# Attention block with an MLP on one core: 128 rows of the second wo tile by an indirect load

## The chip, the core and the metric

The kernel runs on one core of a Trainium2 chip. Its engines are TensorE (PE; PEld is its weight load), VectorE (DVE), ScalarE (ACT), GpSimd (POOL) and SyncE (SP). Transfers between HBM and on-chip memory are carried out by 16 DMA engines, whichever engine issues them. The metric is the time of one execution in device microseconds (us).

## What is computed

A decode step for eight sequences with a cache of keys and values, and an MLP behind it; everything is float32.

```python
mod = (_silu(c) @ w_mod).reshape(8, 6, 1, 512)
sa, ca, ga, sb, cb, gb = (mod[:, i] for i in range(6))
h = _layernorm(x) * (1 + ca) + sa
x = x + ga * attention(h)          # 32 heads, 8 kv heads, the last 2048 cached positions
h = _layernorm(x) * (1 + cb) + sb
x = x + gb * (square(relu(h @ w1 + b1)) @ w2 + b2)

def attention(h):
    q = (h @ wq).reshape(8, 1, 32, 128).transpose(0, 2, 1, 3)
    p = softmax(einsum("bhqd,bhkd->bhqk", q, k) * 128 ** -0.5)   # k, v: repeated for 4 heads
    o = einsum("bhqk,bhkd->bhqd", p, v)
    return o.transpose(0, 2, 1, 3).reshape(8, 1, 4096) @ wo
```

`wo` has 4096 rows of 512 numbers (2 KB a row). Four tiles of 1024 rows each are used, one for every two kv heads.

## The kernel before, in words

The weights and the cache are read once, in a fixed order. A list `loads` (L168 to L175) holds the transfers: the modulation weights, wq, then for each of 16 half heads a K block and a V block of 4 MB each, with the wo tiles put in between, and at the end the last wo tile with w1 and w2. `pump` (L178) issues the head of the list whenever a buffer of its size is free. Four big buffers (32 KB a partition) hold K, V, wq and the tail; one small buffer (16 KB a partition) holds in turn half of the modulation weights, the wo tiles 0 to 2, a part called `far`, and half of w1. `done` (L183) gives a buffer back and calls `pump`. All these transfers are issued by SP and wait on SP for their buffer.

The main loop (L569) has 38 steps. In step `s` VectorE transposes a quarter of a K block (L216), PE makes scores (L387), the softmax runs across several steps, PE multiplies an older V block (`weighted`, L473), and every fourth step `gather` (L508 to L514) writes the attention output of a kv head, transposed, into `oT`. After two kv heads `project_o(j)` (L520) multiplies `oT` with wo tile `j` and adds to `wo_ps`. It stands at steps 14, 22 and 30 for tiles 0 to 2, and behind the loop for the last one.

The rows of a wo tile lie so that a partition holds eight consecutive rows, 16 KB. Tile 0 is different (L128 to L131): of every 32 rows the first 28 are loaded, seven to a partition (14 KB), so that the load has 7/8 of the bytes on every partition. The other 128 rows, four after every 28, are the load `far` (L137 to L144): 32 pieces of 8 KB (four rows). Three transfers on SP put them on a few partitions: twice twelve pieces and once eight. `project_o(0)` does seven products with `oT` and then multiplies the eighth column group of `oT` with a selection matrix `fsel` (L537), which puts the matching outputs on the partitions where the pieces lie; ScalarE copies them to `oX`. `far_rows` (L544) at step 18 multiplies `oX` with the pieces and adds to `wo_ps`. `gather` writes the first two kv heads with two products in place of one (L502 to L506), so that the left-over rows have their own columns.

`fsel` is made at the start by GpSimd (L76 to L85). VectorE's next work there is the selection matrix `sel` (L192).

Behind the loop come the last projection, the second normalisation and the MLP. The products with w2 (L690) follow its four transfers of 8, 4, 1 and 1 chunks (L160); then come two VectorE operations and the store.

Of the kernel before, what the change touches and what calls it, by code (L numbers as in the profile page):

```python
# [8 lines left out]
F32 = mybir.dt.float32  # L9
# [4 lines left out]
EPS = 1e-5  # L14
BIG_SLOTS = 4
PV_LAG = 5


@with_exitstack
def tile_adaln_cached_attention_mlp(  # L20
# [14 lines left out]
    nc = tc.nc  # L35
    P = 128
    B, HKV, SK, DH = k_cache.shape
    D = wq.shape[0]
# [34 lines left out]
    eps = consts.tile([P, 1], F32, name="eps")  # L73
    nc.vector.memset(eps, EPS)
    fsel = consts.tile([P, 4, P], F32, name="fsel")
    nc.gpsimd.memset(fsel, 0.0)  # L76
    for y in range(2):
        nc.gpsimd.tensor_copy(
            fsel[:, :, 32 * y : 32 * y + 12].rearrange("p r (q a) -> p r q a", a=4),
            ident.rearrange("p (y a r q) -> p y r q a", y=2, a=4, r=4)[:, y, :, :3],  # L80
        )
    nc.gpsimd.tensor_copy(
        fsel[:, :, H : H + 32].rearrange("p r (h x) -> p r h x", x=4)[..., 3],
        ident.rearrange("p (h r q) -> p r h q", r=4, q=4)[..., 3],
    )  # L85
    oX = consts.tile([P, 8, 32], F32, name="oX")

# [13 lines left out]
    def load(key):  # L103
        kind, i = key
        held[key] = free[size_of(key)].pop(0)
        if key == ("wq", 0):
            return
        t = slots[size_of(key)][held[key]]
        if kind in "KV":

            hk, c = divmod(i, 2)
            v = k_cache[4 * c : 4 * c + 4, hk] if kind == "K" else v_cache[c::2, hk]
            v = v[:, SK - W :, :].rearrange("u (p j) d -> p u (j d)", j=NJ)
            cuts = (0, big // 2, big) if key == ("V", 2 * HKV - 1) else (0, big)
            for x, y in zip(cuts, cuts[1:]):
                nc.sync.dma_start(t[:, x:y], v[..., x:y])
            return

        def rows(o, v):
            n = v.shape[1] * v.shape[2]  # L120
            nc.sync.dma_start(t[:, o : o + n].rearrange("p (a n) -> p a n", n=v.shape[2]), v)

        w1v = w1.rearrange("(p kc) n -> p kc n", p=P)

        def wo_rows(j):

            r = 2 * REP * DH
            if j == 0:  # L128
                v = wo[:r].rearrange("(b s) n -> b s n", s=32)[:, :28].rearrange("b (g i) n -> b g (i n)", i=7)
                nc.sync.dma_start(t[:, : 7 * D], v)  # L130
                return  # L131
            v = wo[j * r : (j + 1) * r, :].rearrange("(p i) n -> p (i n)", p=P)
            nc.sync.dma_start(t[:, : big // 2], v)

        if kind == "wo":
            wo_rows(i)
        elif kind == "far":  # L137

            nc.gpsimd.memset(t[:H], 0.0)
            v = wo[: 2 * REP * DH].rearrange("(h q s) n -> q h s n", q=4, s=32)[:, :, 28:]  # L140
            v = v.rearrange("q h r n -> q h (r n)")
            for y in range(2):
                nc.sync.dma_start(t[32 * y : 32 * y + 12, : 4 * D], v[:3, 4 * y : 4 * y + 4])
            nc.sync.dma_start(t[3:32:4, 4 * D :], v[3])  # L144
        elif kind == "mod":

            v = w_mod.rearrange("(p kc) n -> p (kc n)", p=P)
            nc.sync.dma_start(t, v[:, big:] if i else v[:, :big])
        elif kind == "wq":

            o = base[held["wq", 0]]
            nc.sync.dma_start(home[:, o : o + 2 * big], wq.rearrange("(p k) n -> p (k n)", p=P))
        elif kind == "tail":
            wo_rows(HKV // 2 - 1)
            rows(big // 2, w1v[:, 0:2])
        elif kind == "w1":
            rows(0, w1v[:, 2:4])
        else:
            v = w2.rearrange("(p c) n -> p c n", p=P)
            for lo, hi in ((0, 8), (8, 12), (12, 13), (13, 14)):  # L160
                rows(D * lo, v[:, lo:hi])
# [5 lines left out]

    loads = [("mod", 0), ("mod", 1), ("wq", 0), ("wq", 1), ("K", 0), ("K", 1)]  # L168
    for n in range(2, 2 * HKV):
        if n == 9:  # L170
            loads.append(("far", 0))
        if n in (4, 11, 13):
            loads.append(("wo", (4, 11, 13).index(n)))
        loads += [("K", n), ("V", n - 2)]
    loads += [("V", 2 * HKV - 2), ("V", 2 * HKV - 1), ("tail", 0), ("w1", 0), ("w2", 0)]  # L175
    at = [0]
# [316 lines left out]
    def gather(hk):  # L493

        o = OS_.pop(hk)
        b = slice(H * (hk % 2), H * (hk % 2) + H)
        pp = ps_m.tile([P, 512], F32, name="m_ps", tag="m_ps")
        for x in range(2):
            to = pp[b].rearrange("p (d x e i) -> p x e d i", x=2, e=2, i=8)[:, x]
            cuts = [(to, o.rearrange("p e (d i) -> p e d i", i=8))]  # L500
            if hk < 2:
                o = o.rearrange("p e (q s) -> p (e q) s", s=32)  # L502
                cuts = [
                    (to[..., :7], o[:, :, :28].rearrange("p a (g i) -> p a g i", i=7)),
                    (to[..., 7].rearrange("p e (r q) -> p e q r", r=4), o[:, :, 28:]),
                ]  # L506
            for dest, src in cuts:
                nc.tensor.matmul(dest, pick[:, x].rearrange("p t u -> p (t u)"), src, start=True, stop=True)  # L508
        tr = work.tile([P, 2, 8, 32], F32, name="tr", tag="b", bufs=1)
        nc.vector.transpose(  # L510
            tr[b].rearrange("p e i (x d) -> p (e i) x d", x=2),
            pp[b].rearrange("p (d x e i) -> p (e i) x d", x=2, e=2, i=8),
        )
        nc.vector.tensor_mul(  # L514
            oT[b, :, :B].rearrange("p i (w e) -> p e i w", e=2),
            tr[b, :, :, :4],
            RZ_[hk][b].rearrange("p (w e) -> p e w", e=2)[:, :, None, :].to_broadcast([H, 2, 8, 4]),
        )

    def project_o(j):  # L520

        last = j == HKV // 2 - 1
        key = ("tail", 0) if last else ("wo", j)
        w = slot(key, D)
        for i in range(8 if j else 7):
            nc.tensor.matmul(
                wo_ps[32 * (i % 4) : 32 * (i % 4) + 32, :],
                oT[:, i, :],
                w[:, i, :],
                start=(j == 0 and i < 4),  # L530
                stop=(last and i >= 4),
            )
        if j == 0:

            px = ps_m.tile([P, 512], F32, name="m_ps", tag="m_ps")
            for r in range(4):
                nc.tensor.matmul(px[:, 32 * r : 32 * r + 32], fsel[:, r], oT[:, 7, :], start=True, stop=True)  # L537
            px = px[:, :P].rearrange("p (r b) -> p r b", b=32)
            nc.scalar.copy(oX[:H, :4], px[:H])
            nc.scalar.copy(oX[:32, 4:], px[H : H + 32])  # L540
        if not last:
            done(key)

    def far_rows():  # L544

        w = slot(("far", 0), D)
        for r in range(8):
            k = H if r < 4 else 32
            nc.tensor.matmul(
                wo_ps[32 * (r % 4) : 32 * (r % 4) + 32, :], oX[:k, r], w[:k, r, :], start=False, stop=False  # L550
            )
        done(("far", 0))

    def late_tiles():

# [12 lines left out]

    for s in range(N + PV_LAG + 1):  # L569
        g, i = divmod(s, C)  # L570
        q, h = divmod(s, 2)
        v = s - PV_LAG
        soft = 1 <= g <= HKV
        ends = v >= C and v % C == 0
        if i == 1 and soft and g < HKV:
            soft_e(g - 1)
        if s < N:
            transposes(q, 2 * h, 0)
        if 1 <= s <= N:
            scores((s - 1) // 2, 2 * ((s - 1) % 2) + 1)  # L580
            if i == 0:
                soft_a(g - 1)
        if s < N:
            transposes(q, 2 * h, 1)
        if i == 1 and soft:
            soft_f(g - 1)
        if v > C and v % (2 * C) == 1 and v < N:
            project_o(v // C // 2 - 1)
        if s == 18:
            far_rows()  # L590
        if 1 <= v <= N:
            weighted(v - 1, 1)
        if i == 0 and soft:
            soft_b(g - 1)
        if s < N:
            transposes(q, 2 * h + 1, 0)
        if i == 1 and soft:
            soft_g(g - 1)
            if g == HKV:
                rT, b1_in, b2_in, x1, h2T = late_tiles()  # L600
        if i == 0 and soft:
            soft_c(g - 1)
        if 1 <= v <= N and v % 2 == 0:
            parts(v // 2 - 1)
        if s < N:
            scores(q, 2 * h)
        if i == 0 and soft:
            soft_d(g - 1)
            if g == HKV:
                soft_e(g - 1)  # L610
        if s < N:
            transposes(q, 2 * h + 1, 1)
        if 0 <= v < N:
            weighted(v, 0)
        if ends:
            gather(v // C - 1)
# [120 lines left out]
```

## Time and profile before

| | |
|---|---|
| Median of three runs | 393.14 us (393.12 to 393.44) |
| The profiled execution | 393.28 us |
| Its span in the trace | 391.5 us |
| TensorE clock granted, mean | 0.886 of full speed |
| Read from HBM | 164.67 MB, 421 GB/s over the span |

The profile is one execution of the kernel. Its page gives each engine's busy time, the span in forty slices, the DMA queues (q1 is SP's, q10 ScalarE's, q8 and q14 carry instructions), the chain of waits that ended last, and the costliest groups of instructions. A group's row has the line, engine, operation and tiles, then the count, the busy time in all and the mean of one in ns, and then the idle time of the engine ahead of it with what ended that. Other views give one stretch of time, one line of the kernel, or the instructions in order; times in them count from the start of the span.

### The profile page before, as it was taken

How to read it: one execution, taken by the hardware profiler on the slowest of the kernel's cores; microseconds unless marked ns; L12 is line 12 of the kernel's file. 1: busy time of each engine (PE TensorE's matmuls, PEld its weight loads, DVE VectorE, ACT ScalarE, POOL GpSimd, SP SyncE). 2: the span in 40 equal slices, each digit the busy share in tenths (PEclk: the TensorE clock that was granted, in tenths of full speed). 3: DMA queues.
4: the chain of work that ended last, by engine and by line, in shares of the span. 5: the costliest groups of instructions: out<-in, count | busy, mean ns of one | idle time of the engine just before them, and what ended most of it. 6: DMA issues, size and time to landing. Idle time of an engine off the chain costs nothing.

```text
span 391.5 us, 4765 instructions
## 1 busy us (share of the span) xinstructions
PE 258.8 (66%) x2050; PEld 79.7 (20%) x2050; DVE 224.0 (57%) x314; ACT 46.7 (12%) x91; POOL 5.9 (2%) x13
## 2 busy tenths in 40 slices
PE   0080959868437873797379828783773737996896
PEld 0030210112112320232122202220221212222333
DVE  1370099878057835874577456490776357854322
ACT  0120111311003100310031003100200003004010
POOL 1000000000000000030000000000000000000000
PEclk9996889998859996999599968988796969997999
DMA  8999999999999999999999999999999999999994
GB/s 330 437 429 426 437 435 442 435 424 411 431 432 432 437 432 435 430 427 429 444 417 435 430 432 432 427 429 427 415 445 437 429 429 431 425 423 424 421 432 190
DMA packets 6915, 165.04 MB, mean 422 GB/s; under 512 B 806, under 2 KB 974, under 8 KB 1230
## 3 DMA queue, kind: packets, MB, share of 16 engines
q1 hardware_dynamic: 6814, 164.70, 98.3%
q8 instruction: 16, 0.26, 0.3%
q10 hardware_dynamic: 80, 0.04, 0.0%
q14 instruction: 5, 0.04, 0.0%
HBM read 164.67 MB, written 0.07 MB: 421 GB/s over the span
## 4 chain that ended last, share of the span: by engine, by line
DMA 59%; DVE 22%; PE 14%; issue 4%; SPq 0%; ACT 0%; DVEq 0%; ACTq 0%
DMA home<-in_A_k_cache_dram 37%; DVE kT L216 12%; DMA home<-in_A_wq_dram 9%; DMA home<-in_B_w_dram 7%; DMA home<-in_A_v_cache_dram 6%; PE s_ps L387 5%; DVE pT L453 4%; PE p_ps L418 3%; PE m_ps L332 2%; PE o_ps L473 2%; DVE pr L446 2%; DVE mx L401 1%; DVE qbd L350 1%; PE m_ps L403 1%; PE m_ps L423 1%
## 5 line engine op out<-in xcount | busy, mean ns | idle before, releaser
L216 DVE STREAM_TRANSPOSE kT<-home 128x1024 f32<-128x1024 f32 x128 | 151.3, 1220 | 81.8 <-DMA home<-in_A_k_cache_dram 77.7
L387 PE MATMUL s_ps<-kT,qst 128*32 128x512 f32 x512 | 129.1, 1075 | 18.9 <-DVE kT L216 18.5
L473 PE MATMUL o_ps<-home,pT 128*32 128x256 f32 x1024 | 70.2, 397 | 11.1 <-DVE pT L453 10.5
L473 PEld LDWEIGHTS o_ps<-home,pT 128*32 128x32 f32 x1024 | 33.8, 118 | 103.1 <-issue 61.3
L403 PE MATMUL m_ps<-ident,mx 128*1 128x128 f32 x16 | 4.3, 364 | 58.3 <-DVE mx L401 58.3
L387 PEld LDWEIGHTS s_ps<-kT,qst 128*32 128x32 f32 x512 | 14.4, 115 | 38.2 <-DVE kT L216 30.1
L453 DVE STREAM_TRANSPOSE pT<-pr 128x2048 f32<-128x2048 f32 x8 | 18.2, 2275 | 1.0 <-ACT pr L436 1.0
L436 ACT ACTIVATE pr<-pr,own 128x512 f32<-128x512 f32 x16 | 17.8, 1223 | 0.3
L430 ACT ACTIVATE pr<-p_ps,nm 128x512 f32<-128x512 f32 x8 | 5.5, 687 | 96.2 <-DVE nm L427 96.2
L397 ACT COPY ss<-s_ps 128x512 f32<-128x512 f32 x8 | 4.7, 586 | 98.1 <-issue 69.2
L332 PE MATMUL m_ps<-home,oX 128*32 128x512 f32 x64 | 9.2, 741 | 10.1 <-DMA home<-in_A_wq_dram 10.1
L375 ACT COPY qst<-q_ps 32x128 f32<-32x128 f32 x32 | 8.2, 256 | 62.9 <-PE q_ps L364 62.6
L350 DVE COPY qbd<-m_ps 32x128 f32<-32x128 f32 x8 | 3.0, 373 | 18.8 <-PE m_ps L347 18.6
L403 PEld LDWEIGHTS m_ps<-ident,mx 128*1 128x1 f32 x16 | 0.7, 81 | 63.5 <-DVE mx L401 63.5
L250 PE MATMUL m_ps<-xsum,sel 128*128 128x1 f32 x2 | 0.6, 362 | 18.5 <-DVE xsum L248 18.5
L418 PE MATMUL p_ps<-ss,perm 128*128 128x512 f32 x16 | 11.8, 829 | 0.0
L427 DVE TENSOR_SCALAR nm<-m_ps 128x1 f32<-128x1 f32 x8 | 1.3, 158 | 16.4 <-PE m_ps L423 16.4
L508 PE MATMUL m_ps<-o_sb,pick 128*64 128x256 f32 (+2 forms) x40 | 9.7, 377 | 0.9 <-DVE o_sb L491 0.9
L446 DVE TENSOR_SCALAR pr<-pr,own 128x512 f32<-128x512 f32 x16 | 9.2, 657 | 0.8 <-ACT pr L430 0.8
L510 DVE STREAM_TRANSPOSE tr<-m_ps 64x512 f32<-64x512 f32 x8 | 5.7, 714 | 5.4 <-PE m_ps L508 5.2
L490 DVE TENSOR_SCALAR o_sb<-o_ps,bit 128x128 f32<-128x128 f32 x16 | 5.2, 327 | 5.5 <-PE o_ps L473 5.4
L228 DVE TENSOR_SCALAR e_sb<-e_sb 128x128 f32<-128x128 f32 x1 | 0.2, 227 | 12.9 <-ACT e_sb L227 12.9
(134 smaller groups left out, 131.7 us busy)
## 6 DMA issues: line engine op xcount, KB each, us to landing
home<-in_A_k_cache_dram SPq DMA_DIRECT2D x16, 4096.0 KB, 36.6
home<-in_A_v_cache_dram SPq DMA_DIRECT2D x15, 4096.0 KB, 22.4
home<-in_w_mod_dram SPq DMA_DIRECT2D x1, 4096.0 KB
small<-in_A_wo_dram SPq DMA_DIRECT2D x2, 2048.0 KB, 25.4
home<-in_A_v_cache_dram SPq DMA_DIRECT2D x2, 2048.0 KB, 21.5
small<-in_w_mod_dram SPq DMA_DIRECT2D x1, 2048.0 KB
home<-in_A_wo_dram SPq DMA_DIRECT2D x1, 2048.0 KB
home<-in_B_w_dram SPq DMA_DIRECT2D x1, 2048.0 KB
```

The lines of the kernel that those rows point to most:

```text
L216: nc.vector.transpose(KTS[q, j][:, rows], k[:, rows, 32 * j : 32 * j + 32])
L332: nc.tensor.matmul(pqs[r][32 * g : 32 * g + 32, :], hT[:, kc, :], w[:, 4 * r + g, :], start=(kc == 0), stop=(kc == NQ - 1),)
L350: nc.vector.tensor_copy(qbd[b, 4 * r : 4 * r + 4, j].rearrange("p g (b t) -> p t g b", t=REP), pT_[b].rearrange("p (t g b) -> p t g b", t= ...
L375: nc.scalar.copy(own[b, :, :, i, 0], pq[b, :P].rearrange("p (c m t) -> p c m t", c=2, t=REP))
L387: nc.tensor.matmul(s_ps[0][32 * g : 32 * g + 32, :], qst[hk % 2][:, P * (4 * c + u) + 32 * j :][:, :32], kT[:, u], start=(c == 0 and j == ...
L403: nc.tensor.matmul(MX_[hk][0:1, :P], mx, ident, start=True, stop=True)
L418: nc.tensor.matmul(sp, perm, SS_.pop(hk), start=True, stop=True)
L436: nc.scalar.mul(X_[hk][..., w], pr, own[:, w : w + 1])
L446: nc.vector.tensor_scalar(X_[hk][..., w], pr, own[:, w : w + 1], None, op0=ALU.mult)
L453: nc.vector.transpose(PT_[hk].rearrange("p e j r -> p j e r"), X_.pop(hk).rearrange("p j x w -> p j (x w)"))
L473: nc.tensor.matmul(O_[n][32 * g : 32 * g + 32, : 2 * DH], PT_[hk][:, e, j : j + 2].rearrange("p j r -> p (j r)"), vt[:, j : j + 2, :].rear ...
L508: nc.tensor.matmul(dest, pick[:, x].rearrange("p t u -> p (t u)"), src, start=True, stop=True)
```

## The change

The second wo tile (`j = 1`) is now laid out like the first: seven rows to a partition by SP, and the other 128 rows apart. These come by one indirect load that GpSimd issues. It takes a row number for each of 128 partitions from `pieces`; wo is seen as 1024 pieces of four rows. On 32 partitions, named by `GROUPS` (eight groups of four), the number is that of a piece; on the other 96 it is 2048, past the end, and these partitions are skipped. The buffer is cleared by GpSimd ahead of it.

```diff
+GROUPS = (64, 96, 68, 100, 92, 124, 16, 28)
...
-    nc.gpsimd.memset(fsel, 0.0)
...
+    oX = consts.tile([P, 8, 32], F32, name="oX")
+    pieces = consts.tile([P, 1], mybir.dt.int32, name="pieces")
+
+    def far_columns():
...
+    def far_groups():
+
+        nc.gpsimd.memset(fsel, 0.0)
+        for h, m in enumerate(GROUPS):
+            nc.gpsimd.tensor_copy(
+                fsel[:, :, m : m + 4], ident.rearrange("p (h r q) -> p h r q", h=8, r=4)[:, h]
+            )
+
+    row = consts.tile([1, P], F32, name="row")
+    nc.gpsimd.memset(row, 4.0 * D)
+    for h, m in enumerate(GROUPS):
+        nc.gpsimd.iota(
+            row[:, m : m + 4],
+            pattern=[[8, 4]],
+            base=2 * P + 32 * h + 7,
+            channel_multiplier=0,
+            allow_small_or_imprecise_dtypes=True,
+        )
+    pr_ = ps_m.tile([P, 512], F32, name="m_ps", tag="m_ps")
+    nc.tensor.matmul(pr_[:, 0:1], row, ones[0:1, 0:1], start=True, stop=True)
+    nc.vector.tensor_copy(pieces, pr_[:, 0:1])
+
+    far_columns()
...
-            if j == 0:
-                v = wo[:r].rearrange("(b s) n -> b s n", s=32)[:, :28].rearrange("b (g i) n -> b g (i n)", i=7)
+            if j < 2:
+                v = wo[j * r : (j + 1) * r].rearrange("(b s) n -> b s n", s=32)[:, :28].rearrange("b (g i) n -> b g (i n)", i=7)
...
+            nc.gpsimd.memset(t[:, : 4 * D] if i else t[:H], 0.0)
+            if i == 0:
+                for y in range(2):
+                    nc.sync.dma_start(t[32 * y : 32 * y + 12, : 4 * D], v[:3, 4 * y : 4 * y + 4])
+                nc.sync.dma_start(t[3:32:4, 4 * D :], v[3])
+            else:
+                nc.gpsimd.indirect_dma_start(
+                    out=t[:, : 4 * D],
+                    out_offset=None,
+                    in_=wo.rearrange("(a r) n -> a (r n)", r=4),
+                    in_offset=bass.IndirectOffsetOnAxis(ap=pieces[:, 0:1], axis=0),
+                    bounds_check=wo.shape[0] // 4 - 1,
+                    oob_is_err=False,
+                )
...
-        if n == 9:
-            loads.append(("far", 0))
-        if n in (4, 11, 13):
-            loads.append(("wo", (4, 11, 13).index(n)))
+        if n in (9, 13):
+            loads.append(("far", n // 13))
+        if n in (4, 11, 14):
+            loads.append(("wo", (4, 11, 14).index(n)))
...
-            if hk < 2:
+            if hk < 4:
...
-        for i in range(8 if j else 7):
+        for i in range(8 if j > 1 else 7):
...
-        if j == 0:
+        if j < 2:
...
+            if j == 0:
+                nc.scalar.copy(oX[:H, :4], px[:H])
+                nc.scalar.copy(oX[:32, 4:], px[H : H + 32])
+            else:
+                nc.scalar.copy(oX[:, :4], px)
...
-    def far_rows():
+    def far_rows(j):
+
+        w = slot(("far", j), D)
+        for r in range(4 if j else 8):
+            k = P if j else H if r < 4 else 32
...
+        done(("far", j))
+        if j == 0:
+            far_groups()
...
-        if s == 18:
-            far_rows()
+        if s in (18, 25):
+            far_rows(s // 25)
```

`far_columns` is the code that made `fsel` before, unchanged. `fsel` is made anew by `far_groups` after the first `far_rows`. In the list of loads the new `far` part stands ahead of the thirteenth pair (K13, V11), and the third wo tile, which was there, ahead of the fourteenth.

More of the change, by code (lines that the diff above doesn't have):

```diff
@@ L75, in tile_adaln_cached_attention_mlp @@
     fsel = consts.tile([P, 4, P], F32, name="fsel")
-    nc.gpsimd.memset(fsel, 0.0)
-    for y in range(2):
+    oX = consts.tile([P, 8, 32], F32, name="oX")
[4 more added lines that the diff above has]
+            nc.gpsimd.tensor_copy(
+                fsel[:, :, 32 * y : 32 * y + 12].rearrange("p r (q a) -> p r q a", a=4),
+                ident.rearrange("p (y a r q) -> p y r q a", y=2, a=4, r=4)[:, y, :, :3],
+            )
         nc.gpsimd.tensor_copy(
-            fsel[:, :, 32 * y : 32 * y + 12].rearrange("p r (q a) -> p r q a", a=4),
-            ident.rearrange("p (y a r q) -> p y r q a", y=2, a=4, r=4)[:, y, :, :3],
-        )
[L82 to L86, printed above, removed]
+            fsel[:, :, H : H + 32].rearrange("p r (h x) -> p r h x", x=4)[..., 3],
+            ident.rearrange("p (h r q) -> p r h q", r=4, q=4)[..., 3],
+        )
+    def far_groups():
+        nc.gpsimd.memset(fsel, 0.0)
+        for h, m in enumerate(GROUPS):
+            nc.gpsimd.tensor_copy(
+                fsel[:, :, m : m + 4], ident.rearrange("p (h r q) -> p h r q", h=8, r=4)[:, h]
[14 more added lines that the diff above has]
+    far_columns()
     big = NJ * DH
@@ L137, in load @@
         elif kind == "far":
-            nc.gpsimd.memset(t[:H], 0.0)
-            v = wo[: 2 * REP * DH].rearrange("(h q s) n -> q h s n", q=4, s=32)[:, :, 28:]
+            r = 2 * REP * DH
+            v = wo[i * r : (i + 1) * r].rearrange("(h q s) n -> q h s n", q=4, s=32)[:, :, 28:]
             v = v.rearrange("q h r n -> q h (r n)")
-            for y in range(2):
-                nc.sync.dma_start(t[32 * y : 32 * y + 12, : 4 * D], v[:3, 4 * y : 4 * y + 4])
-            nc.sync.dma_start(t[3:32:4, 4 * D :], v[3])
+            nc.gpsimd.memset(t[:, : 4 * D] if i else t[:H], 0.0)
+            if i == 0:
+                for y in range(2):
+                    nc.sync.dma_start(t[32 * y : 32 * y + 12, : 4 * D], v[:3, 4 * y : 4 * y + 4])
[8 more added lines that the diff above has]
+                    oob_is_err=False,
+                )
         elif kind == "mod":
@@ L538, in project_o @@
             px = px[:, :P].rearrange("p (r b) -> p r b", b=32)
-            nc.scalar.copy(oX[:H, :4], px[:H])
-            nc.scalar.copy(oX[:32, 4:], px[H : H + 32])
+            if j == 0:
[3 more added lines that the diff above has]
+                nc.scalar.copy(oX[:, :4], px)
         if not last:
             done(key)
-    def far_rows():
-        w = slot(("far", 0), D)
-        for r in range(8):
-            k = H if r < 4 else 32
+    def far_rows(j):
+        w = slot(("far", j), D)
+        for r in range(4 if j else 8):
+            k = P if j else H if r < 4 else 32
             nc.tensor.matmul(
@@ L551, in far_rows @@
             )
-        done(("far", 0))
+        done(("far", j))
+        if j == 0:
+            far_groups()
     def late_tiles():
```

## The prediction

> **What bounds the kernel now.** I read the page first: busy shares, the forty slices, the DMA queues, the chain that ended last.
>
> ```profile
> span 391.5 us, 4765 instructions
> PE 258.8 (66%) x2050; PEld 79.7 (20%) x2050; DVE 224.0 (57%) x314; ACT 46.7 (12%) x91; POOL 5.9 (2%) x13
> DMA  8999999999999999999999999999999999999994
> ...
> q1 hardware_dynamic: 6814, 164.70, 98.3%
> q8 instruction: 16, 0.26, 0.3%
> ...
> DMA 59%; DVE 22%; PE 14%; issue 4%; SPq 0%; ACT 0%; DVEq 0%; ACTq 0%
> ...
> L216 DVE STREAM_TRANSPOSE kT<-home 128x1024 f32<-128x1024 f32 x128 | 151.3, 1220 | 81.8 <-DMA home<-in_A_k_cache_dram 77.7
> ```
>
> No engine is above 66%, the 16 DMA engines are busy in 39 of the 40 slices, and SP's queue (q1) alone fills 98.3% of them. VectorE's transposes waited 77.7 us for K. The kernel is a stream of 165 MB. Next the busy time by stretches, and SP's queue in the long middle one.
>
> ```profile
> 0.00:60.00 60.00, 25.61 (x166) 7.78 (x166) 23.46 (x65) 6.36 (x14) 1.95 (x11) 0.89 0.99 418
> 60.00:350.00 290.00, 201.76 (x1528) 57.90 (x1524) 186.43 (x215) 34.71 (x67) 3.51 (x1) 0.88 1.00 430
> 350.00:383.50 33.50, 26.88 (x251) 11.08 (x248) 13.22 (x32) 5.61 (x10) 0.47 (x1) 0.90 1.00 422
> ```
>
> The last two columns are DMA share and GB/s. The share is 1.00 for 290 us: no engine runs dry, so the stream's end is set by bytes per DMA engine. One engine moves 430/16 = 26.9 GB/s: 8 KB take 0.305 us, 16 KB 0.61 us. The same columns at the end of the stream:
>
> ```profile
> 376.00:383.50 7.50, 7.50 (x46) 2.89 (x46) 2.92 (x11) 0.76 (x3) 0.00 (x0) 1.00 0.98 414
> 384.10:384.80 0.70, 0.70 (x17) 0.44 (x20) 0.00 (x0) 0.00 (x0) 0.00 (x0) 1.00 0.83 342
> 385.10:385.70 0.60, 0.60 (x31) 0.60 (x25) 0.00 (x0) 0.00 (x0) 0.00 (x0) 1.00 0.69 290
> 386.90:387.50 0.60, 0.60 (x32) 0.60 (x28) 0.00 (x0) 0.00 (x0) 0.00 (x0) 1.00 0.27 99
> ```
>
> This is the view on which everything rests. A share of 0.83 is 13 engines of 16, 0.69 is 11. So the engines don't finish together: three are done by about 384.0, two more by about 385.0, and eleven go on. In the last row 0.27 x 0.6 us x 16 = 2.6 engine-us are left for eleven, 0.24 us each: they end at about 387.14. What follows is short:
>
> ```profile
> 338.48 22.42 DMA home<-in_A_v_cache_dram
> 360.97 25.66 DMA home<-in_B_w_dram
> 386.63 0.04 issue
> 386.67 1.76 PE m_ps L690 x48
> ```
>
> The chain of waits ends in the loads of the last V block and of w2. Whatever the eleven late engines gain at the end is gained by the kernel, until the five early ones become late. The most that moving bytes between engines can give is the distance to the mean end: (3 x 384.0 + 2 x 385.0 + 11 x 387.14)/16 = 386.28, that is 0.86 us.
>
> **The change, part by part.** *Bytes.* The second wo load (L133 of before) moved 2048 KB by SP's queue, 128 KB to each engine. Now SP moves 1792 KB, 112 KB to each, and 32 pieces of 8 KB come by one indirect load from GpSimd's queue. Sum of bytes: unchanged. So each engine is relieved of 16 KB, 0.61 us, and gets back 0.305 us for each piece that it carries. If the pieces fall on the five early engines (eight on each of three, four on each of two, which is how eight groups of four partitions would make up these five), the ends become 384.0 - 0.61 + 2.44 = 385.83 for three, 385.0 - 0.61 + 1.22 = 385.61 for two, and 387.14 - 0.61 = 386.53 for eleven. The late eleven still decide: **-0.61 us**. No row shows which engine serves which partition. Bounds: -0.61 if all 32 pieces fall on early engines; 0 if they spread two to each; 8 x 0.305 - 0.61 = +1.83 if eight fall on a late one. I take the first, because three and two is just what the tail shows to be free.
>
> The Trainium skill, page "DMA: Bandwidth & Descriptors", section "The descriptor swizzle", gives a formula of engine by partition for a 128-partition transfer. By it GROUPS puts eight pieces on each of engines 8, 9 and 15 and four on each of 4 and 7, so the sum by it is the -0.61 above. No row here shows engine numbers, and whether it holds for an indirect load with skipped rows isn't shown either.
>
> *The price of a piece on a second queue.* Before has no load by GpSimd. The nearest row is the other queue that breaks into SP's stream with single packets:
>
> ```profile
> q1 hardware_dynamic: 4531, 124.42, 99.9%
> q8 instruction: 12, 0.20, 0.3%
> ```
>
> In this stretch of 290 us, 12 packets of 16 KB took 0.3% of 16 engines: 0.003 x 16 x 290/12 = 1.16 us each, against 0.61 for the same bytes in q1. So a piece costs 0.305 (as q1) to 0.58 us (as q8). At 0.58 the three engines with eight pieces would end at 384.0 - 0.61 + 4.64 = 388.03, 0.9 later than now. I take the low end, plus a little, since q1 itself carries pieces of 8 KB (the first tile's), and an instruction packet goes elsewhere than to the tile; both ends stay in the range. Below nothing a piece can't cost.
>
> *Instruction packets.* The change adds matrix products: one at the start, four with `fsel` and four in `far_rows` for j = 1, two in each of two `gather` calls, minus one in `project_o`: 12, at two PE and two PEld records each (L250's one product stands as x2 of both), 48 records. 4100 PE and PEld records drew the page's 16 q8 packets, one per 256.
>
> ```profile
> q8 instruction: 1, 0.02, 3.5%
> ```
>
> That row is the stretch from 385.5 to 388: the sixteenth packet came at the very end, when five engines were idle. With 48 records more ahead of it, it comes earlier (0.65 us, if the 112 products of L690 run on at 1.95 us for 64), and may meet a working engine. On one of the two with four pieces: 385.61 + 1.16 = 386.77, 0.24 past the late ones. On a late one: +1.16. On one that is done: 0. I take **+0.2**.
>
> *The order of loads.* The far load goes ahead of K13, the third wo tile moves from before K13 to before K14, so its SP issue moves from after V10's to after V11's.
>
> ```profile
> 249.17 1.92 PE L526 MATMUL wo_ps<-small,oT 128*32 128x512 f32 x16
> 261.67 0.54 SPq L116 DMA_DIRECT2D home<-in_A_v_cache_dram  x1
> 262.26 0.58 SPq L133 DMA_DIRECT2D small<-in_A_wo_dram  x1
> 282.60 1.06 PE L473 MATMUL o_ps<-home,pT 128*32 128x256 f32 x16
> 283.72 0.54 SPq L116 DMA_DIRECT2D home<-in_A_v_cache_dram  x1
> ...
> DMA to landing us min/median/max: 20.4/24.4/46.5
> ```
>
> The wo load of 262.26 will stand at about 284.3, behind the V load of 283.72. Meanwhile SP's queue is shorter by 2.1 MB, 4.9 us. Is it ever empty? A K or V load of 4.2 MB takes 9.8 us and lands 20.4 us after its issue at the least, so at least 10.6 us lay ahead of it; 5.7 us remain. Cost 0. POOL's part starts when PE is done with the second tile (about 251.1):
>
> ```profile
> L139 POOL MEMSET small<- 64x4096 f32 x1 | 3.5, 3510 | 168.2 <-PE wo_ps L526 168.2
> L549 PE MATMUL wo_ps<-small,oX x16: 587/600/613, 208.8 to 210.2; 64*32 64x512 f32 x8, 32*32 32x512 f32 x8
> L537 PE MATMUL m_ps<-oT,fsel 128*128 128x32 f32 x8 | 1.1, 279 | 0.0
> L508 PE MATMUL m_ps<-o_sb,pick 128*64 128x32 f32 x4 | 0.5, 208 | 0.0
> ```
>
> The memset of 2048 columns is half of L139's, 1.8 us, so POOL issues the indirect load at about 253. The added wait is PE's: `far_rows(1)` stands ahead of the product of 282.60, 29 us later. Behind it in PE stand V9's products, and behind those SP's V11 load. Until POOL is over 29 us late this costs nothing. No row of before shows POOL making descriptors; SP's issue takes 0.54 us for 128. PE gains eight records at `fsel` (1.1 us), eight in `far_rows` (half of 208.8 to 210.8: 1.0), eight in `gather` (1.0), and loses two: about 3 us in 290 where PE was busy 201.8 and K's landing is what is waited for. ScalarE's copy and POOL's eight small copies at the first `far_rows` lie in idle time. Cost 0; with the cover gone, 3 us.
>
> *The start.*
>
> ```profile
> 1.33 0.19 DVE L192 TENSOR_TENSOR sel<-ident 128x32 f32<-128x32 f32 x1 [0.20 <-POOL ident masks.py:199]
> 1.97 0.46 POOL L78 COPY fsel<-ident 128x48 f32<-128x48 f32 x2
> 15.50 0.23 DVE L228 TENSOR_SCALAR e_sb<-e_sb 128x128 f32<-128x128 f32 x1 [12.86 <-ACT e_sb L227]
> 18.54 0.59 PE L250 MATMUL m_ps<-xsum,sel 128*128 128x1 f32 x2 [18.54 <-DVE xsum L248]
> ```
>
> POOL gets a memset, eight iotas and then the moved copies; PE one product; VectorE waits for it with the `pieces` copy, and `sel` stands behind. Nine small POOL steps at 0.1 to 0.5 us (a copy here is 0.23), 0.6 for the product, 0.2 for the copy: 2 to 6 us. VectorE waits 12.86 us for ScalarE's exponential after that. Cost 0, unless the iotas take over 12 us.
>
> **Sum.** -0.61 + 0.2 = -0.4 us on the profiled execution: its span 391.5 plus 1.8 around it, 393.28, becomes 392.9. The median of the three runs, 393.14, is 0.14 below that execution, so **392.8** as a median.
>
> **Rivals.** *(a) The indirect pieces are dear* (ends slower). The place is the three engines with eight pieces. They have 386.53 - 385.83 = 0.70 us to spare, 0.09 per piece: from 0.40 us a piece on, they end last. At q8's price of 0.58 the result is 394.0; if a break costs twice that excess, 0.85 each, they end at 390.2, 3.1 later, and the time is 396.2. For it: the q8 row. Against: the destination is an ordinary tile. The Trainium skill's same page, section "Latency and other measured facts", calls engines 7 and 15 usually slower and suspects the descriptor rings of loads issued by GpSimd; by it the group of partitions 92 and 124 would be the one late. No run here shows it yet.
>
> *(b) The pieces fall on other engines than the free ones* (slower): +1.83 with eight on a late one, 395.0; +0.61 with four.
>
> *(c) Nothing is rearranged*, the pieces spread evenly: 0, 393.1.
>
> *(d) The instruction packet hits a late engine*: -0.61 + 1.16, 393.7.
>
> *(e) PE waits at `far_rows(1)`* because POOL needs over 29 us: each further us, after 5.7 us of queue, costs one; at 40 us, 398.
>
> **How the numbers follow.** What a measurement of this kernel can tell from no change is about 0.2%, 0.79 us. Forecast 0.43, of which 0.08 is a gain over 0.79 (it needs nearly the whole 0.86, so a luckier place of the instruction packets too). (a) 0.26, of which 0.06 stays within 0.79. (b) 0.14. (c) 0.08. (d) 0.06. (e) 0.03. Faster 0.08; same 0.35 + 0.06 + 0.08 + 0.06 = 0.55; slower 0.20 + 0.14 + 0.03 = 0.37. The range runs from 392.3 (393.14 less 0.86) to 395.0 (case b); above it lie (e) and the dearer half of (a). The likeliest case alone has 392.5 to 393.0.
>
> **What would show it.** Right: a DMA share near 1 until about 385.5, then falling within one us, and the wait of L690 for w2 ending near 386.1 instead of 386.67. Case (a): a few engines still busy after 387.5 at a share of 0.2. Case (b): the share drops to 13 as before and the tail is longer. Case (e): a PE wait on the tile `small`. The forecast is wrong if the share leaves 1.00 anywhere between 60 and 350 us.

## The result, and the profile after

| | before | after |
|---|---|---|
| Median, runs side by side | 393.26 us (393.07 to 393.44) | 394.75 us (394.54 to 394.82) |
| The profiled execution | 393.28 us | 394.81 us |
| Its span in the trace | 391.5 us | 393.0 us |

After is 1.49 us slower: 1.0038 times the time before, 95% interval 1.0026 to 1.0049. The forecast was 392.8.

First the page of after: span, engines, DMA slices, queues, the chain that ended last, VectorE's transposes.

```profile
span 393.0 us, 4840 instructions
...
PE 262.8 (67%) x2074; PEld 82.5 (21%) x2074; DVE 224.0 (57%) x315; ACT 47.1 (12%) x92; POOL 11.3 (3%) x33
...
DMA  8999999999999999999999999999999999999993
...
q1 hardware_dynamic: 6814, 164.43, 97.7%
q8 instruction: 16, 0.26, 0.3%
q0 software_dynamic: 144, 0.26, 0.2%
...
DMA 59%; DVE 22%; PE 14%; issue 4%; SPq 0%; ACT 0%; DVEq 0%; ACTq 0%
...
L256 DVE STREAM_TRANSPOSE kT<-home 128x1024 f32<-128x1024 f32 x128 | 151.3, 1221 | 81.0 <-DMA home<-in_A_k_cache_dram 77.0
```

It is the page of before nearly figure for figure. The chain has the same shares, the transposes wait for K as long, and GpSimd's new queue q0 takes 0.2% of the DMA engines. Nothing here is 1.5 us dearer. The stretches say where it is (the last columns are granted clock, DMA share, GB/s):

```profile
60.00:350.00 290.00, 204.81 (x1550) 59.90 (x1546) 186.67 (x216) 35.09 (x68) 8.10 (x12) 0.89 1.00 430
376.00:383.50 7.50, 7.50 (x46) 2.75 (x45) 2.95 (x12) 0.76 (x3) 0.00 (x0) 1.00 1.00 422
384.10:384.80 0.70, 0.70 (x2) 0.00 (x0) 0.10 (x1) 0.00 (x0) 0.00 (x0) 1.00 0.95 383
385.10:385.70 0.60, 0.00 (x0) 0.00 (x0) 0.00 (x0) 0.00 (x0) 0.00 (x0) 1.00 0.84 324
386.90:387.50 0.60, 0.60 (x32) 0.57 (x23) 0.00 (x0) 0.00 (x0) 0.00 (x0) 1.00 0.09 38
387.50:388.80 1.30, 0.89 (x35) 0.65 (x28) 0.00 (x0) 0.00 (x0) 0.00 (x0) 1.00 0.06 24
```

Up to 383.5 us all is as before: share 1.00 and 430 GB/s in the long middle. Then the tail has changed its shape in two ways. It is fuller: 0.95 where 0.83 stood, 0.84 where 0.69 stood, and only 0.09 instead of 0.27 at 387. The rearrangement did what it was meant to do for most engines. But there is a last row: 0.06 x 1.3 us x 16 = 1.25 engine-us in 1.3 us. That is **one DMA engine, alone**, working when 15 are done. The chain of after ends on it:

```profile
338.81 22.00 DMA home<-in_A_v_cache_dram
360.87 27.24 DMA home<-in_B_w_dram
388.11 0.04 issue
388.15 1.76 PE m_ps L735 x48
```

PE's wait for w2 ends at 388.15 instead of 386.67: +1.48, the whole loss but 0.01. The trace also holds when each of the 16 engines completed its share of the last w2 transfer (us, sorted):

```
before 384.4 384.4 384.6 385.5 385.5 387.4 387.5 387.5 387.5 387.6 387.6 387.6 387.6 387.8 387.8 387.9
after  385.2 385.5 385.9 386.2 386.2 386.7 386.7 386.8 386.9 387.0 387.0 387.1 387.3 387.4 387.7 389.4
```

These completions lie some 1.2 us behind the moment at which the chain lets PE go, because the row of 48 products merges three waits: its first products wait for the transfer of four chunks (last completion 386.6 before, 388.1 after), its last eight for the last transfer. These last eight begin at 387.96 before and at 389.45 after, right behind the completions 387.9 and 389.4. Before: three early, two less early, eleven late, as the shares had said. After: fifteen engines are done by 387.7, 0.2 us before the last of before, and the sixteenth is 1.5 us later than it.

### The profile page after: what moved, and what is told of

It is laid out like the page before. It is cut to its first block, busy times and chain, and to the rows that moved or that the text cites. A ratio compares the mean times of both kernels' runs of the same rounds, so it can differ in the third digit from the quotient of the medians.

```text
span 393.0 us, 4840 instructions
## 1 busy us (share of the span) xinstructions
PE 262.8 (67%) x2074; PEld 82.5 (21%) x2074; DVE 224.0 (57%) x315; ACT 47.1 (12%) x92; POOL 11.3 (3%) x33
## 4 chain that ended last, share of the span: by engine, by line
DMA 59%; DVE 22%; PE 14%; issue 4%; SPq 0%; ACT 0%; DVEq 0%; ACTq 0%
DMA home<-in_A_k_cache_dram 37%; DVE kT L256 12%; DMA home<-in_A_wq_dram 9%; DMA home<-in_B_w_dram 7%; DMA home<-in_A_v_cache_dram 6%; PE s_ps L427 5%; DVE pT L493 4%; PE p_ps L458 3%; PE m_ps L372 2%; PE o_ps L513 2%; DVE pr L486 2%; DVE mx L441 1%; DVE qbd L390 1%; PE m_ps L443 1%; PE m_ps L463 1%
## 5 line engine op out<-in xcount | busy, mean ns | idle before, releaser
L171 POOL MEMSET small<- 64x4096 f32 (+1 forms) x2 | 5.3, 2658 | 242.1 <-PE wo_ps L566 242.1
L548 PE MATMUL m_ps<-o_sb,pick 128*64 128x224 f32 (+2 forms) x48 | 9.9, 345 | 0.9 <-DVE o_sb L531 0.9
```

## The experiments

Two theories stood. (The expectations of e1 to e4 number them A for place and C for price; their B is that an instruction packet made the lone engine late, whatever it carries.) **Place**: one of the three sets of eight pieces fell on an engine that was already late; the price of a piece is as forecast. **Price**: pieces on the second queue are dear wherever they fall, and any engine with eight ends last. A third, smaller question was what the instruction packets do.

**Which set of eight is it?** Each of the first three kernels moves one pair of groups to partitions 48 and 60, which share an engine with 16 and 28 if the forecast's formula holds; in each, then, four sets have eight pieces.

```diff
-GROUPS = (64, 96, 68, 100, 92, 124, 16, 28)
+GROUPS = (48, 60, 68, 100, 92, 124, 16, 28)   e1_pair1
+GROUPS = (64, 96, 48, 60, 92, 124, 16, 28)    e2_pair2
+GROUPS = (64, 96, 68, 100, 48, 60, 16, 28)    e3_pair3
```

> The first eight partitions of GROUPS (64 and 96) are replaced by 48 and 60, so the DMA engine that carried those eight pieces carries none and the two that carried four carry eight. Theory A (eight pieces fell on an engine that was among the eleven late ones: 387.14 - 0.61 + 2.44 = 388.97, the end of the one engine that is busy to 388.8 in the changed kernel): if this pair is the one, the lone engine is gone and the time is 392.7 to 393.1; if not, it stays 394.5 to 394.9. Over the three runs of this kind exactly one is fast. Theory B (the lone engine was hit by an instruction packet at a bad time, whatever it carries): all three stay at 394.5 to 394.9. Theory C (a piece on GpSimd's queue is dear, so any engine with eight is late): all three stay at 394.5 or above, since every one of them leaves engines with eight.

> The same with the second pair (68 and 100) replaced by 48 and 60. Theory A: 392.7 to 393.1 if this pair is the one that fell on a late engine, 394.5 to 394.9 if not. Theories B and C: 394.5 or above.

> The same with the third pair (92 and 124) replaced by 48 and 60. Theory A: 392.7 to 393.1 if this pair is the one that fell on a late engine, 394.5 to 394.9 if not. Theories B and C: 394.5 or above.

Measured, beside before at 393.31 us: e1 394.75 (ratio 1.0039, 1.0025 to 1.0053), e2 **393.03** (0.9992, 0.9983 to 1.0002), e3 394.73 (1.0035, 1.0022 to 1.0047). The last stretch of the three, in this order:

```profile
387.50:388.80 1.30, 0.89 (x35) 0.74 (x32) 0.00 (x0) 0.00 (x0) 0.00 (x0) 1.00 0.07 25
```

```profile
387.50:388.80 1.30, 0.69 (x20) 0.18 (x12) 0.51 (x2) 0.00 (x0) 0.00 (x0) 1.00 0.00 0
```

```profile
387.50:388.80 1.30, 1.30 (x52) 1.05 (x46) 0.00 (x0) 0.00 (x0) 0.00 (x0) 1.00 0.06 24
```

The lone engine (share 0.06 to 0.07) is there with the pair 68 and 100, and gone without it; VectorE is at its last steps then (0.51). Price falls: in e2, by the formula, four engines carry eight pieces each, and none is late. A lone engine that an instruction packet made late would have stayed in e2 as well. The completions of e2 show one thing more: one engine is done at 385.2, the next at 386.3. One engine still has room, and none of these sets falls on it.

**No pieces at all.** The iotas write a number that is past the end everywhere, so that the load transfers nothing.

```diff
-            base=2 * P + 32 * h + 7,
+            base=4 * D + 32 * h + 7,
```

> All 128 row numbers lie past the end, so no piece is loaded and the 128 rows' products are zero: 128 rows of the second wo tile are left out of the result. Every DMA engine has 16 KB less and everything else stands. Theory A: the engines end as in the kernel before, 0.61 us earlier: 392.5 to 392.8. Theory B: the lone engine is still late by an instruction packet, 393.9 to 394.3. Theory C: 392.5 to 393, as A.

Measured: 392.94 us (ratio 0.999, 0.998 to 1.0), -0.37 against before and outside the 392.5 to 392.8 that were expected. Every engine is relieved of 16 KB and gets nothing back; 0.61 was to be had. The 16 completions came at 386.32 in the mean instead of 386.77, and the last at 387.7, 0.2 before that of before (in the profiled execution, which at 393.24 was the slowest of ten). So the relief is real, but smaller than the bytes say; what ate the rest isn't known.

**Half the dose.** Four pieces instead of eight on the engine in question:

```diff
-GROUPS = (64, 96, 68, 100, 92, 124, 16, 28)
+GROUPS = (64, 96, 68, 48, 92, 124, 16, 28)
```

> Of the second pair only the group at 68 stays, the one at 100 goes to 48: the late engine carries four pieces in place of eight. Theory A (eight pieces, 2.44 us, on an engine that was already late): the lone engine ends 1.22 us earlier than in the changed kernel, 394.75 - 1.22 = 393.5 (393.3 to 393.7), half way to the kernel with none on it, 393.03. Theory D (some limit of the indirect load at that place, a threshold and not a sum): 394.75 or 393.0, not between.

Measured: 393.59 us beside 393.38 (1.0006, 0.9996 to 1.0015). The last stretch and the wait:

```profile
387.50:388.80 1.30, 1.30 (x48) 0.98 (x40) 0.00 (x0) 0.00 (x0) 0.00 (x0) 1.00 0.03 11
```

```profile
387.29 1.77 PE m_ps L735 x48
```

The share is 0.03 instead of 0.06, half of one engine's 1.3 us, and the wait ends at 387.29, between the 386.67 of before and the 388.15 of after. The last completion comes at 388.5 with four pieces, at 389.4 with eight: 0.9 us for four more pieces. But the profiled execution of e5, 393.94 us, was the slowest of its ten. By the medians, 394.75 and 393.59, four more pieces cost 1.16 us, 0.29 each, which bears out the forecast's 0.305.

**Another late engine on purpose.** If the formula holds, partitions 4 and 36 belong to an engine that the first tile's far loads have filled.

```diff
-GROUPS = (64, 96, 68, 100, 92, 124, 16, 28)
+GROUPS = (64, 96, 4, 36, 92, 124, 16, 28)
```

> The second pair's eight pieces go to partitions 4 and 36. If the formula of engine by partition holds for the indirect load, this is one of the engines that the first far load, on SP, already filled with nine pieces. Theory A: it's among the late eleven, so it ends 2.44 us later than in the kernel with those pieces on early engines: 394.5 to 395.3. If the pieces of an indirect load fall on engines in another way, 393 to 393.6 is as likely.

Measured: 395.15 us beside 393.38 (1.0043, 1.0026 to 1.006), with a lone engine again:

```profile
387.50:388.80 1.30, 1.13 (x44) 0.86 (x40) 0.00 (x0) 0.00 (x0) 0.00 (x0) 1.00 0.06 22
```

**Two pieces to each engine**, by sixteen groups of two partitions:

```diff
-GROUPS = (64, 96, 68, 100, 92, 124, 16, 28)
+GROUPS = tuple(4 * e for e in range(8)) + tuple(64 + 4 * e for e in range(8))
...
-                fsel[:, :, m : m + 4], ident.rearrange("p (h r q) -> p h r q", h=8, r=4)[:, h]
+                fsel[:, :, m : m + 2],
+                ident.rearrange("p (h r q) -> p h r q", h=8, r=4)[:, h // 2, :, 2 * (h % 2) : 2 * (h % 2) + 2],
...
-            row[:, m : m + 4],
-            pattern=[[8, 4]],
-            base=2 * P + 32 * h + 7,
+            row[:, m : m + 2],
+            pattern=[[8, 2]],
+            base=2 * P + 16 * h + 7,
```

> The 32 pieces are named two to a partition group of four, sixteen groups, so that every DMA engine carries two. Theory A: each engine loses 16 KB and gets 16 KB, so the ends are those of the kernel before: 393.1 to 393.6. Theory C (a piece on the second queue is dearer than in q1, or the skipped rows cost something): every engine pays, over 393.6.

Measured: 393.97 us beside 393.38 (1.0015, 1.0005 to 1.0025), 0.4 above the range expected; by its expectation alone that would speak for dear pieces. But the tail is that of before, as it should be with two pieces to each engine:

```profile
384.10:384.80 0.70, 0.70 (x6) 0.13 (x8) 0.04 (x1) 0.00 (x0) 0.00 (x0) 1.00 0.82 339
385.10:385.70 0.60, 0.60 (x32) 0.60 (x28) 0.00 (x0) 0.00 (x0) 0.00 (x0) 1.00 0.70 290
```

Shares of 0.82 and 0.70 stand where before had 0.83 and 0.69. The store shows that most of the loss lies behind the stream: first this kernel's row in the instructions in order, then that of before.

```profile
389.31 0.35 SPq L746 DMA_DIRECT2D out_dram<-y  x1
```

```profile
389.11 0.35 SPq L700 DMA_DIRECT2D out_dram<-y  x1
```

The store is issued 0.2 us later, but the span is 0.7 longer (392.2 against 391.5). The other 0.5 comes after the store, most of it on GpSimd: its step behind its last drain begins at 391.96, 0.42 us after the drain's end, where before has 0.05. This kernel has eight iotas and eight copies more on GpSimd. What holds it there isn't known. An instruction packet of q14 that only this trace has can't be it, since it starts at about 392.6 us, when the span is over.

**The instruction packets.** Before, with 48 more PE and PEld records in the second tile's projection, and nothing else:

```diff
+        if j == 1:
+            px = ps_m.tile([P, 512], F32, name="m_ps", tag="m_ps")
+            for _ in range(12):
+                nc.tensor.matmul(px[:, :32], fsel[:, 0], oT[:, 7, :], start=True, stop=True)
```

> The kernel before with 12 more products in project_o(1), into a scratch tile that nothing reads: 48 more PE and PEld records and about 3.3 us of PE, nothing else. Theory A: no difference, 393.1 to 393.5. Theory B (instruction packets that come earlier meet a working engine): up to 1.16 later, 393.5 to 394.5.

Measured: 393.39 beside 393.38 us (0.9999, 0.9989 to 1.0009): nothing. Then before with 96 tiny products at the start, enough for a seventeenth packet:

```diff
+    px = ps_m.tile([P, 512], F32, name="m_ps", tag="m_ps")
+    for _ in range(96):
+        nc.tensor.matmul(px[0:1, 0:1], ones[:, 0:1], ones[:, 0:1], start=True, stop=True)
```

> The kernel before with 96 tiny products (one row, one column) put on PE at the very start, where PE waits 18.5 us for its first input: 384 more PE and PEld records, 1.5 instruction packets of 256. Nothing reads the result. If an instruction packet takes its DMA engine's time as q8's 1.16 us says, and the late engines are late by such packets, one engine gets a 17th packet before the end of the stream and ends last by itself: 394.2 to 394.9, with a DMA share near 0.06 at the end. If instruction packets cost the stream nothing (they slip in between), or the extra one meets an early engine: 393.1 to 393.6.

Measured: 393.58 us beside 393.35 (1.0011, 1.0001 to 1.0022), scattered from 393.25 to 395.45. The packet is there, on the page, and the profiled execution of 395.31 us has a lone engine at the end:

```profile
q8 instruction: 17, 0.28, 0.3%
```

```profile
386.90:387.50 0.60, 0.60 (x20) 0.60 (x16) 0.00 (x0) 0.00 (x0) 0.00 (x0) 0.50 0.29 109
387.50:388.80 1.30, 1.30 (x32) 1.30 (x28) 0.00 (x0) 0.00 (x0) 0.00 (x0) 0.50 0.05 20
```

But the clock column reads 0.50 there, where it reads 1.00 in the other kernels: its products ran at half speed at the very end, and the last eight began at 389.90, 0.9 us after the last completion (389.0). So the time of this execution says nothing on the packet. The completions do: 389.0 is 1.1 us later than the last of before, and it is one engine alone. In the executions down to 393.25 us no engine can have been that late; why isn't known.

**Who filled the late engines?** Before without the three SP loads that bring the 128 far rows of the first tile:

```diff
-            for y in range(2):
-                nc.sync.dma_start(t[32 * y : 32 * y + 12, : 4 * D], v[:3, 4 * y : 4 * y + 4])
-            nc.sync.dma_start(t[3:32:4, 4 * D :], v[3])
```

> The kernel before without the three SP loads of the first tile's far pieces (the buffer is cleared, so these 128 rows' products are left out of the result). Three engines carried nine of these pieces each, five carried one. If these three are among the eleven late engines, eleven become eight: the DMA share between 385.1 and 385.7 falls from 0.69 to 0.5 or less, and the time stays within 0.4 of before (392.9 to 393.4), since the other late engines decide. If the eleven are late for another reason, the share stays near 0.69.

Measured: 393.22 us (0.9998, 0.9988 to 1.0007). The time doesn't move, but the tail does:

```profile
384.10:384.80 0.70, 0.70 (x32) 0.70 (x28) 0.00 (x0) 0.00 (x0) 0.00 (x0) 1.00 0.68 275
385.10:385.70 0.60, 0.60 (x31) 0.52 (x20) 0.00 (x0) 0.00 (x0) 0.00 (x0) 1.00 0.55 212
```

0.68 against 0.83 and 0.55 against 0.69, about two engines of 16 in each stretch. The completions count it better: eight come from 387.3 on, not eleven. So three of the eleven were late by the first tile's far rows; the other eight are late for something else, and the end is theirs.

**What filled the other eight?** The same trace tells. Every transfer ends with a packet of 4 bytes on each of the 16 engines, and how far these lie apart is how far the engines have drifted apart. Six transfers of the long middle, with the time of the first of these packets, the number of 16 KB instruction packets (q8) that had come by then, and the delay of the last eight engines behind the first (us, sorted):

```
 75.3   1   0.41 0.44 0.49 0.51 0.60 0.64 1.49 1.97
 85.0   2   0.41 0.44 0.51 0.60 0.64 1.49 1.97 2.04
108.7   3   0.43 0.51 0.61 0.64 1.50 1.79 1.96 2.04
137.8   4   0.52 0.62 0.66 1.51 1.79 1.89 1.98 2.05
167.0   5   0.62 0.66 1.51 1.79 1.89 1.98 2.00 2.05
176.7   6   0.67 1.52 1.79 1.82 1.89 1.97 2.00 2.05
```

Each packet adds one engine to those that are 1.7 us or more behind, and the engine stays behind. (The one at 1.5 was there before the first packet.) The trace of before gives the same counts. The packet itself takes 1.0 to 1.1 us, and the stream's next packet on that engine often 1.7 instead of 1.2, some 1.5 us in all. At 351.9 us six engines are 3.0 to 3.3 behind, two 1.5 and the other eight 1.2 or less; two more packets follow, and at the end eight engines are some 3 us behind (387.3 to 387.6 against 384.4), as two packets each would make them. So instruction packets filled the other eight. Fifteen had come, which is one short of two for each; as far as the order of the delays tells, the eighth owes its delay to 8 KB instruction packets of q14.

**The placement of e2 once more**, with more rounds:

> The changed kernel with the pair 68 and 100 replaced by 48 and 60 once more, in more rounds, since it is the version that may beat both kernels: 392.9 to 393.2, 0.2 to 0.4 below before. If the first three rounds were chance, it is within 0.1 of before.

Measured: **392.93 us** beside 393.35 (0.999, 0.9981 to 0.9999), 0.42 below before and 1.8 below after; its slowest run, 393.07, lies below the fastest of before, 393.19. Its tail and its wait:

```profile
384.10:384.80 0.70, 0.70 (x25) 0.65 (x28) 0.00 (x0) 0.00 (x0) 0.00 (x0) 1.00 1.01 415
385.10:385.70 0.60, 0.60 (x31) 0.60 (x24) 0.00 (x0) 0.00 (x0) 0.00 (x0) 1.00 1.00 362
386.90:387.50 0.60, 0.60 (x28) 0.42 (x16) 0.00 (x0) 0.00 (x0) 0.00 (x0) 1.00 0.03 10
```

```profile
360.49 25.76 DMA home<-in_B_w_dram
386.29 1.74 PE m_ps L735 x48
```

A share of 1 until 385.7, then a fall within about a us, and the wait of the last products ends at 386.29: nearly what the forecast had named as its sign (386.1).

## Why the prediction was wrong

**What bounds the kernel** was right: the end is that of the latest DMA engine, and 1.48 of the 1.49 us lie in the wait for w2.

**Bytes: this step failed.** It took -0.61 on the ground that all 32 pieces fall on the five early engines, "because three and two is just what the tail shows to be free". The tail shows how many engines are free, not which. Two of the three sets of eight, and both sets of four, lay well; the set on partitions 68 and 100 lay on one of the eleven late ones. The step had this as its upper bound, +1.83 (388.97 for that engine's end), and the rival on other engines had it at 395.0 with a chance of 0.14; measured were 394.75, +1.49. The 0.34 less than the bound fits an engine that was not the last of the eleven: one that completes at 389.4 with +1.83 would have completed at 387.6 before, where the last came at 387.9. No run names that engine in before, so this is argued. The sign that the forecast gave for this rival, a share that drops to 13 engines as before, didn't come: the share stood at 0.95 there, since the other sets lay well, and only the tail was longer.

The match of three and two came from the Trainium skill's formula ("DMA: Bandwidth & Descriptors", section "The descriptor swizzle"), which gives engine by partition. The formula itself isn't at fault: e1, e2, e3, e5 and e8 come out as it says (394.75, 393.03, 394.73, 393.59 and 395.15 us), for an indirect load with skipped rows too, though no run shows an engine's number. What it could not tell was which engines the rest of the stream had left free. By e10 that is set by the first tile's far rows on three engines and by instruction packets on eight; the engine of 68 and 100 was among these eleven.

**The price of a piece** was right at its low end. The queues of after while the load ran, 257 to 270 us:

```profile
q1 hardware_dynamic: 175, 5.21, 93.4%
q0 software_dynamic: 144, 0.26, 5.3%
q8 instruction: 1, 0.02, 0.5%
```

0.053 x 13 us x 16 = 11.0 engine-us for 32 pieces, 0.34 each with all that is small in that queue, below the 0.40 at which the rival of dear pieces began; the packet records have 0.31 to 0.32 us for each piece alone. e2 and e11 settle it: four engines with eight each, and faster. That rival's other support, the Trainium skill's remark (same page, "Latency and other measured facts") that engines 7 and 15 are usually slower, has none here: in e2, by the formula, engines 7 and 15 carry eight pieces each, no engine is late, and the time is 393.03.

**The instruction packets** were put at +0.2, for a sixteenth packet that comes earlier and may meet a working engine. No run shows that cost: e7's 48 records cost nothing, and the sixteenth packet of after starts at 386.9 us, not earlier than the 386.0 of before. The price of a packet, 1.16 us, was too low by the delay of the packet behind it (1.5 in all), and the larger effect was missed: it is these packets that had filled eight of the late engines.

**The order of loads** cost nothing, as forecast. The instructions of after in order:

```profile
250.83 1.80 POOL L171 MEMSET small<- 128x2048 f32 x1 [74.73 <-PE wo_ps L566]
252.93 1.17 POOL L177 DMA_INDIRECT small<-in_A_wo_dram,pieces  x1 [0.29 <-POOL small L171]
```

```profile
282.88 1.06 PE L592 MATMUL wo_ps<-small,oX 128*32 128x512 f32 x8
```

The memset took 1.80 us (1.8 forecast), the indirect load left at 252.93 (about 253), and the product in `far_rows(1)` came 30 us later with no wait in its row. PE's busy time between 60 and 350 us grew from 201.76 to 204.81, the 3 us of the forecast, and the DMA share there stayed 1.00.

**The start** cost nothing either:

```profile
1.66 0.68 POOL L104 IOTA row<- 1x4 f32 x8
2.40 0.58 PE L112 MATMUL m_ps<-ones,row 1*128 1x1 f32 x2 [2.40 <-POOL row L104]
3.02 0.16 DVE L113 CAST pieces<-m_ps 128x1 int32<-128x1 f32 x1 [1.87 <-PE m_ps L112]
3.09 0.28 DVE L232 TENSOR_TENSOR sel<-ident 128x32 f32<-128x32 f32 x1
15.50 0.23 DVE L268 TENSOR_SCALAR e_sb<-e_sb 128x128 f32<-128x128 f32 x1 [11.29 <-ACT e_sb L267]
```

`sel` moved from 1.33 to 3.09, VectorE's wait for the exponential shrank from 12.86 to 11.29, and the step behind it starts at 15.50 as before.

So with one pair of numbers in `GROUPS` changed e11 measured -0.42, and the forecast was -0.4. That agreement is partly luck: the relief was less than the 0.61 of the sum (e4, with nothing put back, gained 0.37), and the +0.2 for packets that took the sum to -0.4 isn't in any run. Not settled: where the rest of the 0.61 went, why e9 lost time in some of its executions only, and which engine is the one that e2 leaves with room.

## What to carry to other kernels

A DMA share of 13/16 at the end of a saturated stream tells how many engines are free and not which; before bytes are placed by hand, find which places are free by moving one group at a time, as e1 to e3 do. The two sides aren't alike: the best placement can gain only the distance to the mean end (0.86 us by the forecast, of which 0.42 was got), while one misplaced set costs nearly its full time (+1.5 with the other sets well placed). Look for the loss in the last 2 us: a share of 0.06 for 1.3 us is one engine of 16, which no average over the span shows.

## What the runs showed of the hardware

A row that an indirect load skips isn't free of packets: q0 has 144 packets for 32 pieces, the other 112 of 4 bytes, 9 ns each but one in the packet records; in e4, where all 128 rows are skipped, all 144 are of 4 bytes. On engines that carry eight pieces these alternate one by one with SP's packets from 257.7 to 268 us, so both queues move on together. GpSimd's issue for 128 row numbers took 1.17 us. An instruction packet of 16 KB that falls into a saturated stream puts its DMA engine some 1.5 us behind the others, and it stays behind: in e10 one, two, up to six engines are 1.7 us or more behind the first after one, two, up to six packets. And time can be lost after the last store: e6 lost some 0.5 us there, more than its tail did.
